# Reordering one DMA-issuing queue in a fused linear-attention and Mish-MLP kernel

## The chip, the cores and the metric

The kernel runs on one core of a Trainium2 chip. A core has a matrix engine (PE, TensorE), a vector engine (DVE, VectorE), an activation engine (ACT, ScalarE), a general engine (POOL, GpSimd) and an engine that here only issues transfers (SP, SyncE). Each engine works through its own queue of instructions in order; an instruction that needs a result of another engine or of a transfer (a DMA) waits at the head of its queue, and everything behind it on that engine waits as well. SP, ACT and POOL issue DMAs. The metric is the device time of one execution in microseconds.

## The reference

Attention with a per-head decay `lam`, computed block by block with a running state, and then a two-layer network. There are 4 batches, 8 heads, 768 positions and a head size of 64.

```python
for b in range(nb):
    sl = slice(b * block, (b + 1) * block)
    qb, kb, vb = (q[:, :, sl].copy(), k[:, :, sl].copy(), v[:, :, sl].copy())
    intra = np.einsum('bhic,bhjc->bhij', qb, kb) * Dmask[None]
    intra = np.einsum('bhij,bhjd->bhid', intra, vb)
    inter = np.einsum('bhid,bhde->bhie', qb * lam_pow[None], kv_state)
    out[:, :, sl] = intra + inter
    rev_pow = lam[:, None, None] ** (block - 1 - pos[None, :, None])
    kb_dec = kb * rev_pow[None]
    kv_state = lam_block[None, :, None, None] * kv_state + np.einsum('bhsd,bhse->bhde', kb_dec, vb)
...
h = x @ w_in
sp = np.where(h > 20.0, h, np.log1p(np.exp(np.minimum(h, 20.0))))
g = h * np.tanh(sp)
return (g @ w_out).astype(np.float32)
```

`x` holds the attention's output as 3072 tokens by 512 features; `w_in` is 512 x 2048 and `w_out` 2048 x 512. `g` is the Mish function of `h`.

## The kernel before, in words

**Stages.** The 768 positions are cut into NG = 6 groups of C = 128. Group n has B = 4 chunks, one for each batch, numbered i = 4n + b. Stage n of the main loop (line 800) does the two matrix layers for the 512 tokens of group n and, in between, the attention of group n + 1, in pairs of chunks: pair `s` (batches 0 and 1) and pair `t` (batches 2 and 3). Group 0 and the attention of group 1 are done ahead of that loop.

**Units.** A stage is a list of units of PE work written out by hand. For n > 1 there are 27: units 0 to 12 are the first layer (products `ph`, and for the last 1024 hidden features a scheme with seven half-size products, whose tiles appear as `sx`, `sz`, `sw`, `sy`), and units 13 to 26 are the second layer, in seven steps of two units each: P1 (13, 14), P5 (15, 16), P6 (17, 18), P2 (19, 20), P7 (21, 22), P3 (23, 24) and P4 (25, 26), with the tiles `x`, `w`, `z`, `x`, `z`, `y`, `z`. Stage 1 has 16 units of the first layer, so that its P1 is 16 and 17 and its P4 28 and 29. After each unit's PE work the loop body places other engines' work, in program order; this order is the order of each engine's queue.

**The path of one chunk.** `load_k`, `load_q` and `load_v` are DMAs issued by POOL (lines 66 to 78), one in each unit of `slots`, each behind a tiny copy (`pace`, line 408) that waits for the newest activation output. `scale_k` (line 262) multiplies a chunk of k by its decay on DVE and gives `ktil`. `turn` (line 269) calls `scale_k` and then issues two DMA transposes on SP: `qraw` from `qn` and `kraw` from `ktil`. `pair_s` (line 338) makes the scores of two chunks on PE (`pS`) and masks them on DVE (`sb`, line 365). `pair_o` (line 368) makes the outputs on PE and scales them into `xtok`: for pair `t` at once on DVE (line 385), for pair `s` later on ACT (line 389), from the list `scales`, whose four entries are taken in units 15, 16, 17 and 19. After the second half of each chunk's `xtok` SP issues the DMA transpose into `xt` (line 392), the input of the first layer in the next stage. `pair_a` (line 320) updates the running state (`raw`, line 288, and `state`, line 293).

**The readers of `xt`.** In stage n the units 0 to 3 use only the half of `xt[n]` that pair `s` gave. The half of pair `t` is first read by `x_sum(n, 0)` on DVE (line 519), placed in unit 3 ahead of `pair_s` on `s`, and by PE from unit 4 on.

**The stores.** P2 and P4 store through ACT's queue. P7 and P3 end in `plus` (line 651): DVE adds two halves into `osum` (line 654), and SP issues the store at once. The `osum` tiles rotate through 4 buffers (tag `osb`).

**Buffers that bear on the order.** `kn` has 6 buffers, `qn` 5, `ktil` 6, `qraw` and `kraw` 4 each.

**SP's queue in a stage with n = 2 or 3**, in program order: turns of chunks 4(n+1)+2 and 4(n+1)+3 (units 1 and 2); transposes into `xt` of pair `s` (units 16 and 19); turn of chunk 4(n+2) (unit 20); store of P7 (22); turn of chunk 4(n+2)+1 (23); store of P3 (24); transposes into `xt` of pair `t` (25). In stage 4 the turns of units 20 and 23 are absent, since there is no further group.

Of the kernel before, what the change touches and what calls it, by code (L numbers as in the profile page):

```python
# [13 lines left out]
def bc(ap, axis, n):  # L14
    shape = list(ap.shape)
    shape.insert(axis, n)
    return ap.unsqueeze(axis).broadcast_to(shape)
# [3 lines left out]
def kernel(  # L21
# [10 lines left out]
    nc = tc.nc  # L32
    B, H, S, D = q.shape
    C = 128
    NG = S // C
# [41 lines left out]
    def load_v(i):  # L77
        nc.gpsimd.dma_start(out=vz[i % NVB][:, :, 0:D], in_=chunk_rows(v, i))  # L78
# [119 lines left out]
    ktil = {}  # L198
# [27 lines left out]
    def look_s(i):  # L226

        kT, qT = kq[i]
        pS = [ps.tile([128, JP, C], F32, name="pS", tag=g, bufs=m)
              for g, m in (("pS", 1), ("po", 2) if i < B else ("pk", 1))]  # L230
        for j in range(JP):
            for t in range(2):
                rs = slice(64 * t, 64 * t + 64)
                nc.tensor.matmul(pS[t][:, j, :], kT[rs, j, :], qT[rs, j, :],
                                 start=(j == 0), stop=(j == JP - 1), skip_group_check=True)
        sbs[i] = [None, None]
        for t in (0, 1) if i < B else (1, 0):
            sbs[i][t] = work.tile([128, JP, C], F16, name="sb", tag="sb", bufs=4)
            nc.vector.tensor_tensor(out=sbs[i][t], in0=pS[t],
                                    in1=dm[:, t] if i < B else bc(maskT, 1, JP), op=ALU.mult)  # L240
# [21 lines left out]
    def scale_k(i):  # L262

        t = work.tile([128, H, D], F16, name="ktil", tag="ktil", bufs=6)
        (nc.gpsimd if B + 1 < i < 2 * B else nc.vector).tensor_tensor(  # L265
            out=t, in0=kn[i], in1=bc(lk, 2, D), op=ALU.mult)
        ktil[i] = t

    def turn(i):

        scale_k(i)
        for src, name, to in ((qn, "qraw", qraw), (ktil, "kraw", kraw)):
            to[i] = work.tile([128, JP, C], F16, name=name, tag=name, bufs=4)
            nc.sync.dma_start_transpose(out=to[i], in_=src[i].rearrange("p h c -> p (h c)"))
# [16 lines left out]
    def next_state(n, p):  # L291

        nc.vector.tensor_tensor(
            out=state[p][(n + 1) % 2], in0=raws[n, p],
            in1=lbc.unsqueeze(1).unsqueeze(3).broadcast_to([128, 2, JP, D]), op=ALU.mult)
# [112 lines left out]
    def pace():  # L408
        nc.gpsimd.tensor_copy(paced, mark[-1])  # L409
# [188 lines left out]
    def token_sum(n, i, part):  # L598

        if (n, i) not in gsum:  # L600
            gsum[n, i] = work.tile([128, HK, 2 * C], F16, name=f"gsum{i}", tag=f"gsum{i}", bufs=1)
        w = HK // 2
        ks = slice(part * w, part * w + w)
        kh = slice(HK + part * w, HK + part * w + w)
        h = hsg[n]
        lo, hi = slice(0, 2 * C), slice(2 * C, 4 * C)
        a, b, op = (
            lambda: (h[:, ks, hi], h[:, kh, hi], ALU.add),
            lambda: (gsum[n, 0][:, ks, :], h[:, ks, lo], ALU.subtract),
            lambda: (h[:, ks, lo], h[:, ks, hi], ALU.subtract),  # L610
            lambda: (h[:, kh, lo], gsum[n, 1][:, ks, :], ALU.subtract),
        )[i]()
        nc.vector.tensor_tensor(out=gsum[n, i][:, ks, :], in0=a, in1=b, op=op)  # L613
# [31 lines left out]
    def store(n, r, c, t, queue, blk=None, lo=0, hi=None):  # L645
        hi = HN if hi is None else hi
        b0, b1 = (2 * r, 2 * r + 2) if blk is None else (2 * r + blk, 2 * r + blk + 1)
        dst = out_v[n * C : (n + 1) * C, b0:b1, c * HN + lo : c * HN + hi]
        queue.dma_start(out=dst, in_=t)

    def plus(n, r, c, key):

        o = work.tile([128, 2, HN], F32, name="osum", tag="osb", bufs=4)
        nc.vector.tensor_tensor(out=o, in0=bank[n, key], in1=p5[n], op=ALU.add)  # L654
        store(n, r, c, o, nc.sync)

    p5 = {}
    u3 = []

# [140 lines left out]
    for n in range(1, NG):  # L800
        r, s, t = Pair(), Pair(), Pair()
        r.n, r.bs, s.n, s.bs, t.n, t.bs = n, (2, 3), n + 1, (0, 1), n + 1, (2, 3)
        def duo(g, half):
            return mm1_duo, (n, g, half * (GT // 2), (half + 1) * (GT // 2))

        def part(g, *steps):
            return [(set_unit, (n, g, step)) for step in steps]

        later = []
        if 1 < n < NG - 1:  # L810
            later += [lambda i=(n + 1) * B + b: load_v(i) for b in range(B)]
        if n < NG - 2:
            later += [lambda f=f, i=(n + 2) * B + b: f(i) for b in range(B) for f in (load_k, load_q)]
        if n == 1:
            units = [[duo(g, half)] for half in range(2) for g in range(NKI // 2)]
            visit = {11: (pair_s, s), 16: (pair_o, s), 21: (pair_a, s), 26: (pair_s, t), 29: (pair_o, t)}
            turns = {1: 9, 4: 10, 7: 11, 23: 12, 25: 13}
            slots = range(8, 16)
            sums = {9: ((2, 0),), 11: ((2, 1),), 13: ((0, 0), (1, 0)), 15: ((0, 1), (1, 1)), 20: ((3, 0),), 21: ((3, 1),)}
        else:  # L820
            units = [part(0, "P1") + part(1, "P1") + [duo(0, 0)], part(0, "P2") + part(1, "P2") + [duo(1, 0)],
                     [duo(2, 0)], [duo(3, 0)],
                     [duo(0, 1)], part(0, "open") + [duo(1, 1)], part(1, "open") + [(mm1_duo, (n, 2, GT // 2, GT, True))],
                     part(0, "P5") + [(duo_mish, (n, 2, 1))] + part(1, "P5"), part(0, "P6", "mid") + part(1, "P6"), [duo(3, 1)] + part(1, "mid"),
                     part(0, "P7") + part(1, "P7"), part(0, "P3") + part(1, "P3"),
                     part(0, "P4") + part(1, "P4") + part(0, "late") + part(1, "late")]
            if n == NG - 1:
                units[0] += units[1].pop(),
            visit = {}
            if n < NG - 1:  # L830
                visit = {0: (pair_a, r), 3: (pair_s, s), 13: (pair_o, s), 22: (pair_s, t), 25: (pair_o, t)}
            if n < NG - 2:
                visit[17] = pair_a, s
            turns = {1: (n + 1) * B + 2, 2: (n + 1) * B + 3, 20: (n + 2) * B, 23: (n + 2) * B + 1}
            slots = range(4, 16)
            sums = {9: ((2, 0),), 12: ((0, 0), (0, 1), (1, 0), (1, 1)), 14: ((2, 1),), 18: ((3, 0),), 19: ((3, 1),)}
        steps = ("P1", "P5", "P6", "P2", "P7", "P3", "P4")
        units += [[(fast_unit, (n, step, blk))] for step in steps for blk in range(2)]
        scales = []
        for u, calls in enumerate(units):  # L840
            for fn, args in calls:
                fn(*args)
            if n == 1 and u == 0:
                turn(8)
                look_s(7)
            if n == 1 and u == 2:
                f = look_kv(7)
                look_o(7)
                f()
                next_state(1, 1)  # L850
            for _ in range({0: 1, 1: 1, 2: 2, 3: 1, 4: 1}.get(u, 0) if n == 1 else 0):
                pace()
                ahead.pop(0)()
            if later and u in slots:
                pace()
                later.pop(0)()
            for i, part in sums.get(u, ()):
                token_sum(n, i, part)
            if turns.get(u, NG * B) < NG * B:
                turn(turns[u])  # L860
            if n > 1 and u == 3:
                x_sum(n, 0)
            if u in visit:
                f, s_ = visit[u]
                s_.spare = ("po", "po") if u < 13 else ("pS", "pk") if f is pair_a else ("ph", "po")
                if f is pair_o and s_ is s and n > 1:
                    f(s_, scales)
                else:
                    f(s_)
            if n > 1 and scales and u in (15, 16, 17, 19):  # L870
                scales.pop(0)()
            if n > 1 and u == 4:
                for i in range(1, 4):
                    x_sum(n, i)
# [30 lines left out]
```

## Time and profile before

| What | Value |
|---|---|
| Timed runs | 199.07, 199.34, 200.79 us (median 199.34) |
| The profiled execution's own time | 198.38 us |
| Its span in the profile | 196.6 us |
| PE idle, recorded waits from 57 to 196.6 us | one, 0.3 us |
| SP, waits of stores for `osum` | 69.5 us in 6, the longest 41.9 |
| DVE, waits of `xsum` for the DMA into `xt` | 4.3 us in 2, the longest 3.6 |

The span is what the profile covers, from the first instruction to the last; the execution's own time has 1.78 us around it. SP's waits are the waits of an issuing queue, which are free unless something behind the waiting transfer is needed. How to read the rows of the profile: a timeline row has the start and the duration in us, the engine (SPq is SP's queue, with issue time as its duration), the line of the kernel, the operation, the output tile and its inputs, the shapes, how many instructions the row merges, and in brackets the idle time ahead of it and what ended that. A row on landing gives the smallest, middle and largest time from a DMA's issue until its data is there.

### The profile page before, as it was taken

What the parts mean: (1) busy time and instruction counts of PE and PEld (TensorE: products, weight loads), DVE (VectorE), ACT (ScalarE), POOL (GpSimd) and SP (SyncE); (2) the same over time, 40 slices, a digit from 0 to 9 for tenths busy, and PEclk for the clock granted to TensorE, in tenths of its full rate; (3) what the DMA queues carried; (4) which work ended last, traced back from release to release, by engine and by line L of the source; (5) the groups of instructions that cost most, each with busy time, mean ns of one, the idle gap of its engine ahead of it and who ended that gap; (6) DMA issues with size and microseconds to landing.
All of it is one profiled execution on the core that took longest, in us unless ns stands there. A gap on an engine that the chain in (4) does not pass through costs nothing.

```text
span 196.6 us, 5100 instructions
## 1 busy us (share of the span) xinstructions
PE 189.4 (96%) x2049; PEld 157.8 (80%) x2049; DVE 145.2 (74%) x279; ACT 110.7 (56%) x230; POOL 78.7 (40%) x129
## 2 busy tenths in 40 slices
PE   7978999999999999999999999999999999999993
PEld 3654447978888998988998988998987988888882
DVE  8789689899944978898769798769788728227813
ACT  5695674333665521567880657980647880787520
POOL 7996333679487800008970008960007000000000
PEclk9999999999999999999999999999999999999999
DMA  8999999999999997759999959999969914600014
GB/s 127 141 144 200 207 205 207 155 174 212 198 128 161 179 137 170 182 89 94 129 120 196 216 107 111 121 122 159 218 136 103 62 27 137 160 3 2 0 57 160
DMA packets 112458, 26.82 MB, mean 136 GB/s; under 512 B 101554, under 2 KB 112434, under 8 KB 112434
## 3 DMA queue, kind: packets, MB, share of 16 engines
q0 software_dynamic: 77552, 13.37, 93.2%
q1 hardware_dynamic: 30848, 9.97, 28.8%
q10 hardware_dynamic: 4034, 3.15, 5.7%
q8 instruction: 16, 0.26, 0.6%
q14 instruction: 8, 0.07, 0.1%
HBM read 27.26 MB, written 6.29 MB: 171 GB/s over the span
## 4 chain that ended last, share of the span: by engine, by line
PE 74%; DMA 11%; POOL 8%; DVE 4%; issue 1%; ACT 1%; POOLq 0%; DVEq 0%; ACTq 0%
PE ph L453 19%; PE z L627 14%; DMA wout<-in_moe_w_out_dram 10%; PE x L627 9%; PE y L627 6%; PE sz L579 5%; PE w L627 4%; PE sx L579 3%; PE pS L349 2%; PE pO L376 2%; POOL win L93 2%; POOL vz L78 2%; PE sy L579 2%; PE sw L579 2%; POOL kn L67 1%; POOL qn L75 1%
## 5 line engine op out<-in xcount | busy, mean ns | idle before, releaser
L453 PE MATMUL ph<-xt,win 128*128 128x256 f16 x384 | 45.0, 273 | 0.0
L453 PEld LDWEIGHTS <-win 128*128 128x128 f16 x384 | 37.1, 98 | 5.0 <-issue 0.2
L627 PEld LDWEIGHTS <-gsum 128*128 128x128 f16 x384 | 36.9, 98 | 4.5
L465 ACT ACTIVATE hsg<-ph 128x512 f16<-128x512 f32 x48 | 28.6, 596 | 14.8 <-PE ph L453 14.6
L409 POOL COPY paced<-hsg 1x1 f16<-1x1 f16 x42 | 9.8, 234 | 55.3 <-ACT hsg L465 55.3
L627 PEld LDWEIGHTS <-hsg 128*128 128x128 f16 x272 | 26.0, 98 | 3.2
L627 PE MATMUL x<-wout,hsg 128*128 128x256 f16 x192 | 23.7, 273 | 0.0
L627 PE MATMUL z<-tsum,gsum 128*128 128x256 f16 x192 | 23.6, 273 | 0.0
L613 DVE TENSOR_TENSOR gsum<-hsg 128x1024 f16<-128x1024 f16 x24 | 16.1, 686 | 9.6 <-ACT hsg L540 4.7
L78 POOL DMA_DIRECT2D vz<-in_v_dram x24 | 21.1, 881 | 4.9 <-DMA wout<-in_moe_w_out_dram 1.7
L67 POOL DMA_DIRECT2D kn<-in_k_dram x23 | 20.5, 892 | 6.1 <-DMA win<-in_moe_w_in_dram 2.2
L75 POOL DMA_DIRECT2D qn<-in_q_dram x23 | 20.4, 885 | 6.0 <-DMA wout<-in_moe_w_out_dram 3.6
L365 DVE TENSOR_TENSOR sb<-pS,maskT 128x512 f16<-128x512 f32 x32 | 19.8, 682 | 0.5 <-PE pS L349 0.3
L684 ACT ACTIVATE osum<-z 128x512 f32<-128x512 f32 x5 | 3.0, 597 | 25.1 <-PE z L627 25.1
L265 DVE TENSOR_TENSOR ktil<-kn,lk 128x512 f16<-128x512 f16 (+1 forms) x22 | 14.6, 683 | 2.2 <-DMA kn<-in_k_dram 2.2
L288 DVE TENSOR_TENSOR raw<-pv,state 64x256 f32<-64x256 f32 x24 | 10.1, 422 | 7.8 <-PE pv L328 7.4
L418 PE MATMUL ph<-xt,win 128*128 128x512 f16 x64 | 14.5, 379 | 0.3 <-ACT xt L257 0.3
L579 PEld LDWEIGHTS <-isum 128*128 128x128 f16 x128 | 12.5, 98 | 2.0 <-issue 0.5
L430 ACT ACTIVATE hsg<-ph 128x512 f16<-128x512 f32 x16 | 9.6, 597 | 5.8 <-PE ph L418 5.8
L418 PEld LDWEIGHTS <-win 128*128 128x128 f16 x64 | 6.1, 98 | 7.3 <-DMA win<-in_moe_w_in_dram 0.5
L654 DVE TENSOR_TENSOR osum<-z,p 128x512 f32<-128x512 f32 x6 | 4.1, 690 | 10.6 <-issue 5.9
L627 PE MATMUL y<-wout,gsum 128*128 128x256 f16 x96 | 11.8, 273 | 0.0
(113 smaller groups left out, 314.6 us busy)
## 6 DMA issues: line engine op xcount, KB each, us to landing
vz<-in_v_dram POOLq DMA_DIRECT2D x24, 128.0 KB, 4.6
out_dram<-osum SPq DMA_DIRECT2D x12, 256.0 KB, 3.3
kn<-in_k_dram POOLq DMA_DIRECT2D x23, 128.0 KB, 5.3
qn<-in_q_dram POOLq DMA_DIRECT2D x23, 128.0 KB, 5.9
out_dram<-osum ACTq DMA_DIRECT2D x11, 256.0 KB, 3.1
wout<-in_moe_w_out_dram POOLq DMA_DIRECT2D x4, 512.0 KB, 16.4
win<-in_moe_w_in_dram POOLq DMA_DIRECT2D x3, 512.0 KB, 10.1
win<-in_moe_w_in_dram POOLq DMA_DIRECT2D x2, 256.0 KB, 6.2
```

What stands on the lines that cost most here:

```text
L67: nc.gpsimd.dma_start(out=kn[i], in_=chunk_rows(k, i))
L75: nc.gpsimd.dma_start(out=qn[i], in_=chunk_rows(q, i))
L78: nc.gpsimd.dma_start(out=vz[i % NVB][:, :, 0:D], in_=chunk_rows(v, i))
L265: (nc.gpsimd if B + 1 < i < 2 * B else nc.vector).tensor_tensor(out=t, in0=kn[i], in1=bc(lk, 2, D), op=ALU.mult)
L288: nc.vector.tensor_tensor(out=raw[rs, b % 2, j0 : j0 + nj, :], in0=pv[rs, :, rs], in1=olds(rs), op=ALU.add)
L365: nc.vector.tensor_tensor(out=s.sb[m][t], in0=sc[m][t], in1=bc(maskT, 1, JP), op=ALU.mult)
L418: nc.tensor.matmul(ph_t[ni][:, lo:hi], w_in(ni, kc), xt[n][:, kc, lo:hi], start=(kc == 0), stop=(kc == NKC - 1),)
L453: nc.tensor.matmul(t[:, m, lo - half * h : hi - half * h], w_in(ni, kc), xt[n][:, kc, lo:hi], start=(m == 0 and kc == 0), stop=(kc == NKC ...
L465: nc.scalar.activation(dst, duo_t[n, g, half], AF.Mish)
L579: nc.tensor.matmul(t[:, m, :], lhs(kk, m), rhs(kk), start=(step in ("P1", "P5") and m == 0 and kk == 0), stop=(kk == KH - 1), skip_group_c ...
L613: nc.vector.tensor_tensor(out=gsum[n, i][:, ks, :], in0=a, in1=b, op=op)
L627: nc.tensor.matmul(places(n, key)[:, blk, lo:hi], lhs(kk, blk), rhs(kk, lo, hi), start=(fresh and kk == 0 and blk == 0), stop=(kk == HK - ...
```

## The change

- `turn` no longer scales k if the chunk was scaled already.
- In stages 1 to 4 the stores of P7 and P3 are put on a list, `owed`, and issued at the end of the body of unit 25 (unit 29 in stage 1), behind `pair_o` of pair `t` and so behind its two transposes into `xt`. Stages 0 and 5 keep the old order.
- The loads of group n + 2 come in the order k, k, q, q for batches 0 and 1 and then for 2 and 3, instead of k, q, k, q.
- The turns of the next group's first pair move from units 23 and 25 to 20 and 22 in stage 1, and from 20 and 23 to 19 and 20 in stages 2 and 3.
- In stages 2 and 3 `scale_k` of that pair is placed in unit 15, both chunks together.
- The entries of `scales` are taken ahead of the turn and the visit of their unit instead of behind them, so that in unit 19 the last transpose into `xt` of pair `s` still comes ahead of the turn.

```diff
     def turn(i):
-        scale_k(i)
+        if i not in ktil:
+            scale_k(i)
...
         nc.vector.tensor_tensor(out=o, in0=bank[n, key], in1=p5[n], op=ALU.add)
-        store(n, r, c, o, nc.sync)
-
+        if 0 < n < NG - 1:
+            owed.append(lambda: store(n, r, c, o, nc.sync))
+        else:
+            store(n, r, c, o, nc.sync)
+
+    owed = []
...
         if n < NG - 2:
-            later += [lambda f=f, i=(n + 2) * B + b: f(i) for b in range(B) for f in (load_k, load_q)]
+            later += [lambda f=f, i=(n + 2) * B + b + c: f(i)
+                      for b in (0, 2) for f in (load_k, load_q) for c in range(2)]
...
-            turns = {1: 9, 4: 10, 7: 11, 23: 12, 25: 13}
+            turns = {1: 9, 4: 10, 7: 11, 20: 12, 22: 13}
...
-            turns = {1: (n + 1) * B + 2, 2: (n + 1) * B + 3, 20: (n + 2) * B, 23: (n + 2) * B + 1}
+            turns = {1: (n + 1) * B + 2, 2: (n + 1) * B + 3, 19: (n + 2) * B, 20: (n + 2) * B + 1}
...
                 token_sum(n, i, part)
+            if n > 1 and scales and u in (15, 16, 17, 19):
+                scales.pop(0)()
+            if n > 1 and u == 15 and n < NG - 2:
+                scale_k((n + 2) * B)
+                scale_k((n + 2) * B + 1)
             if turns.get(u, NG * B) < NG * B:
                 turn(turns[u])
...
-            if n > 1 and scales and u in (15, 16, 17, 19):
-                scales.pop(0)()
+            if u == (29 if n == 1 else 25):
+                while owed:
+                    owed.pop(0)()
```

## The prediction, made before the change was run

> **What bounds the kernel now.** I read the page's busy times and slices first, to learn which engine is full, then busy time by stage, then the chain of waits around the one stage that differs from its neighbours, and last the queues of SP, DVE and POOL there.
>
> ```profile
> span 196.6 us, 5100 instructions
> PE 189.4 (96%) x2049; PEld 157.8 (80%) x2049; DVE 145.2 (74%) x279; ACT 110.7 (56%) x230; POOL 78.7 (40%) x129
> PE   7978999999999999999999999999999999999993
> ...
> 80.50:109.60 29.10, 29.10 (x347) 25.86 (x345) 23.89 (x46) 17.88 (x43) 12.50 (x24) 1.00 1.34 143
> 109.60:138.65 29.05, 29.05 (x346) 25.82 (x345) 23.55 (x45) 18.19 (x43) 12.39 (x24) 1.00 1.52 141
> 138.65:167.90 29.25, 28.87 (x339) 25.38 (x337) 20.58 (x40) 17.98 (x43) 4.57 (x8) 1.00 0.71 105
> ```
>
> TensorE (PE) is busy in every slice from the fourth to the last but one, and the granted clock is 1.00 in the stretches. The three stretches are the stages n = 2, 3 and 4; columns are length, then busy time of PE, weight load, DVE, ACT, POOL, then the granted clock. Stages 2 and 3 have no PE idle time at all. Nothing that SP, DVE or POOL does can make a stage shorter than PE's own work, and the change takes no PE instruction away. So the whole possible gain is the PE time lost in stages 1 to 4. Stage 4 has 0.38 us of it (29.25 - 28.87), although it has less to do: it has no state update for the next pair (`pair_a` on `s` stands only where n < 4). To size the loss I compare like with like, from each stage's first matmul (`sx`) to the first product of the second half (`x`), which hold the same units in stages 3 and 4. The columns of the chain of waits are start, duration, what:
>
> ```profile
> 109.59 0.87 PE sx L579 x8
> ...
> 124.15 0.87 PE x L627 x8
> ...
> 138.65 0.87 PE sx L579 x8
> ...
> 142.55 2.45 DMA xt<-xtok
> ...
> 147.53 0.60 ACT sz L559
> 148.13 0.52 ACT hsg L465
> 148.70 0.60 PE sw L579 x4
> ...
> 153.84 0.87 PE x L627 x8
> ```
>
> Stage 3 takes 124.15 - 109.59 = 14.56 us, stage 4 takes 153.84 - 138.65 = 15.19: **0.63 us lost**. The chain names the path: the second half of `xt` is transposed by a DMA that lands at 145.00 (142.55 + 2.45), `x_sum` on DVE waits for it, the four masked scores `sb` are queued behind `x_sum`, ACT's copy `sz` waits for the bank that `sb` reads, the Mish `hsg` is queued behind that copy, and PE's `sw` waits for the bank that this Mish empties.
>
> **The change part by part.** *Stores behind the outputs' transposes, and the next pair's transposes in one piece (turns at units 19 and 20).* SP's queue at the end of stage 3, and the DVE work that feeds it:
>
> ```profile
> 133.54 1.20 SPq L274 DMA_TRANSPOSE qraw<-qn  x1
> ...
> 136.15 0.54 SPq L649 DMA_DIRECT2D out_dram<-osum  x1
> 136.79 1.22 SPq L274 DMA_TRANSPOSE qraw<-qn  x1
> 138.10 1.21 SPq L274 DMA_TRANSPOSE kraw<-ktil  x1
> 139.40 1.75 SPq L649 DMA_DIRECT2D out_dram<-osum  x1
> 141.25 2.52 SPq L392 DMA_TRANSPOSE xt<-xtok  x2
> ...
> 138.09 1.40 DVE L385 TENSOR_TENSOR xtok<-pO,lqt 128x256 f16<-128x256 f32 x4
> ...
> 143.05 1.28 DVE L265 TENSOR_TENSOR ktil<-kn,lk 128x512 f16<-128x512 f16 x2
> 145.09 0.42 DVE L519 TENSOR_TENSOR xsum<-xt 128x512 f16<-128x512 f16 x1 [0.76 <-DMA xt<-xtok]
> 145.55 2.48 DVE L365 TENSOR_TENSOR sb<-pS,maskT 128x512 f16<-128x512 f32 x4
> ```
>
> The first `xtok` is ready after two of DVE's four, at about 138.09 + 0.70 = 138.79, but SP issues its transpose at 141.25: it stands behind a transpose that ends at 139.31 and a store that takes 1.75. After the change SP runs four transposes in a row from 133.54, each about 1.3 from start to start (136.79 to 138.10), so the fourth ends at about 133.54 + 3 x 1.3 + 1.21 = 138.65. The outputs' transposes then start at 138.8 and 140.1 instead of 141.25 and 142.55, that is 2.45 us sooner. With the landing of 2.45 from the chain, `xt` is there at about 142.55. DVE gets to `x_sum` when `ktil` ends, 143.05 + 1.28 = 144.33, so the wait is gone with 1.8 us to spare.
>
> What is late next is `sb`. In stage 3, where `x_sum` waits for nothing, it starts as soon as PE has written the scores:
>
> ```profile
> 115.20 0.62 PE L349 MATMUL pS<-qraw,kraw 64*128 64x128 f16 x16
> 144.27 0.62 PE L349 MATMUL pS<-qraw,kraw 64*128 64x128 f16 x16
> ...
> 115.86 2.48 DVE L365 TENSOR_TENSOR sb<-pS,maskT 128x512 f16<-128x512 f32 x4
> ```
>
> There `sb` starts 0.66 after the first score matmul; in stage 4 that would be 144.93 instead of 145.55, 0.62 sooner. That is the 0.63 by another road, and beyond it PE sets the start. So this term is **-0.63 us**, in stage 4 alone: in stages 2 and 3 PE loses nothing now. The two stores cost SP the same issue time later, behind the outputs' transposes; queued behind them are only the transposes for units 1 and 2 of the next stage, whose scores PE reads at unit 22. In stage 4 that is well after the `x` of unit 13 at 153.84, while SP is done with `xt` at 143.77 (141.25 + 2.52) even now: over 10 us of cover for a delay of 1 or 2. Each stage takes four `osum` buffers and there are four, so a store held back to unit 25 is waited for by the same step one stage on. Cost 0.
>
> *k decays moved, k ahead of q.* In stages 2 and 3 the two `scale_k` go from units 20 and 23 to unit 15 on DVE. No instruction is added. The stage 2 rows:
>
> ```profile
> 97.98 0.68 DVE L613 TENSOR_TENSOR gsum<-hsg 128x1024 f16<-128x1024 f16 x1
> 100.18 1.75 DVE L288 TENSOR_TENSOR raw<-pv,state 64x256 f32<-64x256 f32 x4 [1.51 <-PE pv L328]
> ...
> 102.57 1.29 DVE L613 TENSOR_TENSOR gsum<-hsg,gsum 128x1024 f16<-128x1024 f16 x2
> 103.78 0.68 DVE L265 TENSOR_TENSOR ktil<-kn,lk 128x512 f16<-128x512 f16 x1
> ...
> 93.44 0.87 POOL L67 DMA_DIRECT2D kn<-in_k_dram  x1
> 94.42 0.87 POOL L75 DMA_DIRECT2D qn<-in_q_dram  x1
> 95.69 0.88 POOL L67 DMA_DIRECT2D kn<-in_k_dram  x1 [0.23 <-issue]
> ...
> DMA to landing us min/median/max: 4.1/4.3/4.9
> ```
>
> DVE is idle for 1.51 us before `raw`, and the two decays (1.28 for a pair, by the `ktil` row above) fit into it: 98.6 to 99.9, ahead of 100.18. The new wait is for the loads. The first k is issued at 93.44 as before; the second takes q's slot at 94.42 instead of 95.69. The last row above is the k loads' time to landing in stage 2 (4.1 to 4.9), so they are there by 98.3 and 99.3, when DVE comes for them or before. With the old order the second would land at up to 100.6 and hold `raw`. Queued behind the wait on DVE are `raw`, the state and `gsum`, and PE needs that `gsum` for step P3. Cost 0, bounded above in the second rival; below, two instructions leave a stretch of DVE that is full (103.78 on), which saves nothing on PE's path. At n = 1 the turns only come sooner (units 20 and 22) and their decays fall into DVE's idle time ahead of `raw` and `osum` of that stage: 0. ACT's scaled outputs keep their order on ACT and on SP (they are popped ahead of the turn of unit 19 instead of ahead of that of unit 20): 0.
>
> **The sum.** -0.63 + 0 + 0 = -0.63. The profiled execution took 198.38 us (span 196.6 and 1.78 around it) and becomes 197.75. The three timed runs have their median at 199.34, 0.96 above the profiled one, with the same program, so I take the same difference off it: **198.7**.
>
> **Rivals.** *First: the transposes land no sooner.* Landing, not issue, may be the limit, since six transposes now follow each other with an ACT store beside them. The rows for the outputs' transposes (from 80 to 170 us) and for the q transposes issued at 133.54 and 136.79:
>
> ```profile
> DMA to landing us min/median/max: 2.4/2.5/3.4
> ...
> DMA to landing us min/median/max: 4.9/4.9/4.9
> ```
>
> At 4.9 the second output transpose, issued at 140.1, lands at 145.0, exactly as now, and the gain is 0: 199.3. From 4.2 down (144.3) the gain is whole. All the output transposes so far landed within 3.4, those right behind a store among them, which speaks for the gain; that q's took twice as long while the DMA engines were loaded speaks for the rival. The Trainium skill has a rule on this side (DMA: Bandwidth & Descriptors, "Issuing engines are not separate DMA queues"): DMAs from all queues run on the same 16 engines and interleave, and starting them from several queues saves only issue time. Taken strictly, with the engines full, a sooner issue lands no sooner and the sum is 0; the landings of 2.4 to 3.4 behind a store lean against that reading here. Chance 0.25.
>
> *Second: DVE stands at the early decays (slower).* If the second k lands late, DVE holds everything behind it. After the landing come the decay (0.60, half of a pair less its overlap), `raw` and the state (102.57 - 100.18 = 2.39) and two `gsum` (1.29), 4.3 us together, and PE wants the last of it in the first P3 product, which runs from 105.52:
>
> ```profile
> 105.52 1.85 PE y L627 x16
> ```
>
> Half of that product's 0.9 needs only the first `gsum`, so the deadline is about 105.9 and the k must be there by 101.6, 7.2 us after its issue at 94.42. The latest k in stage 3 took 6.6:
>
> ```profile
> DMA to landing us min/median/max: 4.0/4.3/6.6
> ```
>
> so no k load of these stages would have reached that point; each us beyond it costs PE one, in stage 2 and again in stage 3. The weights' loads early in the run took longer:
>
> ```profile
> win<-in_moe_w_in_dram POOLq DMA_DIRECT2D x3, 512.0 KB, 10.1
> ```
>
> At the 10.1 of that row the loss would be 2 x 2.9 = 5.8 and the time 199.34 - 0.63 + 5.8 = 204.5; at 8.7 it would be 3.0, or 201.7. No weights are loaded in these stages, so chance 0.07.
>
> *Third: timed runs lose more than the profiled one.* They lie between 199.07 and 200.79; if the excess is the same wait for `xt` recurring in other stages, the change takes off up to the 199.34 - 198.38 = 0.96 as well, 0.63 + 0.96 = 1.6 in all: 197.8. Nothing in the profile shows such waits (stages 2 and 3 are full). Chance 0.08, with 0.03 of it for more than that, as only the slowest timed run lies far enough above the profiled one (2.41) to hold it.
>
> **How the numbers follow.** The forecast, 198.7, has 0.60; no gain, 199.3, 0.25; slower by DVE's wait 0.07; the larger gain 0.08. The range runs from the larger gain, 197.8, to 200.3, which is no gain plus two thirds of what the slowest timed run lies above the median (1.45), as medians of few runs move. That leaves out the slow rival and the far end of the larger gain, about 1 in 10, and some of the runs' own spread. About 1% (2 us) is what a measurement of this kernel can tell from no change. Faster by over 1% needs under 197.35, a gain of 2.0 where the profile has 0.63 to give: 0.03. Slower by over 1% is the second rival, 0.07. Within 1%: 0.90.
>
> **What would show it.** Right: on SP four transposes in a row from about 133.5, `xt` issued near 138.8, both stores behind; no DVE wait of `xsum` for `xt` in stage 4, no PE wait of `sw` there, and sx to x in 14.56. For the k decays: two `ktil` ahead of `raw` in stages 2 and 3, with at most tenths of idle time for the loads. Wrong: `xt` landing 4 us or more after its issue, DVE idle on `kn` for over 2 us, or a PE wait in a stage that has none now.

## The result, and the profile after

| | Median | Runs | Range |
|---|---|---|---|
| Kernel before | 199.17 us | 19 | 198.14 to 201.58 |
| Changed kernel | 198.46 us | 19 | 197.63 to 199.40 |

The ratio is 0.9956, with a 95% interval of 0.9936 to 0.9977: the change takes off 0.9 us, with 0.5 to 1.3 us inside the interval. The ratio leaves out the run of 201.58 us, which counts as a slow one; the medians differ by 0.71 us. The forecast was 198.7 us, a gain of 0.63; the measured median lies 0.24 us below it.

The profiled execution of the changed kernel took 198.19 us (span 196.4). Its page says the same of PE as before, one percentage point fuller:

```profile
span 196.4 us, 5097 instructions
PE 189.9 (97%) x2049; PEld 158.3 (81%) x2049; DVE 144.8 (74%) x279; ACT 110.8 (56%) x230; POOL 79.0 (40%) x129
```

By this page the span fell by only 0.2 us. The stages tell where the rest is. The view of busy time by stretches, cut at each stage's first `sx`, has length, then busy time of PE, weight load, DVE, ACT and POOL, then the granted clock:

```profile
80.99:110.06 29.07, 29.07 (x347) 25.84 (x345) 24.46 (x48) 17.85 (x43) 12.71 (x24) 1.00 1.35 143
110.06:139.12 29.06, 29.06 (x346) 25.80 (x345) 23.58 (x46) 18.17 (x43) 12.60 (x24) 1.00 1.48 143
139.12:167.75 28.63, 28.63 (x339) 25.41 (x337) 20.03 (x39) 18.02 (x43) 4.46 (x8) 1.00 0.68 101
```

Stages 2 and 3 are as long as before. Stage 4 took 29.25 us (138.65 to 167.90) and now takes 28.63, with no idle time of PE left in it: 0.62 us gained (29.25 - 28.63). Against that, this execution reached stage 2 at 80.99 us, where the profile of before had 80.52: 0.47 us lost in the part before it. The tail of stage 5 gives 0.05, and -0.62 + 0.47 - 0.05 is the -0.20 of the span. The part ahead of stage 2 varies by itself: two profiles of the kernel before reached stage 2's first `sx` at 80.52 and 81.41, two of the changed kernel at 80.99 and 80.55. So one pair of spans says little here, and the stages' own lengths say much.

In the chain of waits (start, duration, what) the half of stage 4 from `sx` to `x` is now as long as that of stage 3, 14.57 us each, and no DMA, DVE or ACT step stands between the two in stage 4:

```profile
110.06 0.87 PE sx L580 x8
...
124.63 0.87 PE x L628 x8
...
139.12 0.87 PE sx L580 x8
...
153.69 0.87 PE x L628 x8
```

The timelines of SP's queue and of DVE at the same place (line numbers of the changed kernel are one higher around here):

```profile
134.60 1.20 SPq L275 DMA_TRANSPOSE qraw<-qn  x1
136.30 1.20 SPq L275 DMA_TRANSPOSE kraw<-ktil  x1
137.61 1.19 SPq L275 DMA_TRANSPOSE qraw<-qn  x1
138.90 1.22 SPq L275 DMA_TRANSPOSE kraw<-ktil  x1
140.21 3.19 SPq L393 DMA_TRANSPOSE xt<-xtok  x2
143.45 1.09 SPq L650 DMA_DIRECT2D out_dram<-osum  x2
...
143.52 1.29 DVE L265 TENSOR_TENSOR ktil<-kn,lk 128x512 f16<-128x512 f16 x2
144.74 0.43 DVE L520 TENSOR_TENSOR xsum<-xt 128x512 f16<-128x512 f16 x1
145.40 2.48 DVE L366 TENSOR_TENSOR sb<-pS,maskT 128x512 f16<-128x512 f32 x4 [0.23 <-PE pS L350]
```

Four transposes run in a row (with 0.50 us between the first two), both stores stand behind the outputs' transposes, `xsum` follows `ktil` with no wait for a DMA, and `sb` waits for PE's scores and for nothing else. But the two output transposes take 3.19 us of SP where they took 2.52. The first alone holds SP for 1.88, and the second starts at 142.18:

```profile
140.21 1.88 SPq L393 DMA_TRANSPOSE xt<-xtok  x1
...
142.18 1.22 SPq L393 DMA_TRANSPOSE xt<-xtok  x1
```

The early decays stand where they were meant to, in the idle time ahead of `raw`, with no wait for a load (DVE in stage 2):

```profile
99.06 1.29 DVE L265 TENSOR_TENSOR ktil<-kn,lk 128x512 f16<-128x512 f16 x2
100.65 0.42 DVE L289 TENSOR_TENSOR raw<-pv,state 64x256 f32<-64x256 f32 x1 [0.30 <-PE pv L329]
```

### The profile page after: what moved, and what is told of

The parts are those of the page before. It is cut to its first block, busy times and chain, and to the rows that moved or that the text cites. A ratio compares the mean times of both kernels' runs of the same rounds, so it can differ in the third digit from the quotient of the medians.

```text
span 196.4 us, 5097 instructions
## 1 busy us (share of the span) xinstructions
PE 189.9 (97%) x2049; PEld 158.3 (81%) x2049; DVE 144.8 (74%) x279; ACT 110.8 (56%) x230; POOL 79.0 (40%) x129
## 4 chain that ended last, share of the span: by engine, by line
PE 93%; ACT 2%; DVE 2%; issue 1%; ACTq 0%
PE ph L454 22%; PE z L628 15%; PE x L628 11%; PE ph L419 7%; PE y L628 6%; PE sz L580 5%; PE w L628 5%; PE sx L580 4%; PE pS L350 2%; PE pO L377 2%; PE pO L255 2%; PE sy L580 2%; PE sw L580 2%; PE pS L234 1%; PE pv L329 1%; PE busy L157 1%
```

## The experiments

Theory A is the prediction's: SP's issue of two stores ahead of the outputs' transposes holds `xt`, which reaches PE through DVE's queue in stage 4, and nothing else in the change matters. Theory B gives the gain to the earlier turns and decays. Theory C says that timed runs lose more than the profile shows. Ratios are to the kernel before, run on the same chip between the others.

### One part alone: the stores held back

```diff
-        store(n, r, c, o, nc.sync)
+        if 0 < n < NG - 1:
+            owed.append(lambda: store(n, r, c, o, nc.sync))
+        else:
+            store(n, r, c, o, nc.sync)
...
+            if u == (29 if n == 1 else 25):
+                while owed:
+                    owed.pop(0)()
```

> The kernel before with one part of the change alone: the stores of P7 and P3 are held back behind the outputs' transposes in stages 1 to 4. Theory A (SP's issue of the two stores ahead of the outputs' transposes is the whole cost): without them the transposes into xt go out 1.5 to 2.5 us sooner, stage 4 from its first sx to its first x takes 14.6 instead of 15.19 us, PE has no wait in stage 4, and the ratio to the kernel before is about 0.997 (-0.6 us). Theory B (the earlier turns and decays make the gain): stage 4 keeps its 15.2 and the ratio is 1.000.

Measured: ratio 0.9985 (0.9964 to 1.0006), median 198.53 against 198.93. In its chain of waits stage 4 runs from 139.37 to 153.94:

```profile
139.37 0.87 PE sx L579 x8
...
153.94 0.87 PE x L627 x8
```

That is 14.57 us, and PE has no wait in stage 4: this part alone brings stage 4 to the length that the whole change gives it. The outputs' transposes start 0.33 us after the stage's `sx`, where they started 2.60 after it before (141.25 - 138.65) and 1.09 after it in the changed kernel (140.21 - 139.12):

```profile
139.70 3.45 SPq L392 DMA_TRANSPOSE xt<-xtok  x2
```

The timed ratio allows for no gain as well as for 0.63 us (0.997); the stage decides it.

### All parts but that one

```diff
-        if 0 < n < NG - 1:
-            owed.append(lambda: store(n, r, c, o, nc.sync))
-        else:
-            store(n, r, c, o, nc.sync)
+        store(n, r, c, o, nc.sync)
```

> The changed kernel with the stores of P7 and P3 issued at once, as before: turns, decays and order of loads stay changed. Theory A: SP gets through its four transposes sooner but still issues two stores ahead of the transposes into xt, the second with about 1.75 us; stage 4 from sx to x takes 15.0 to 15.2 us and the ratio to the kernel before is 0.999 to 1.000. Theory B: 14.6 us and 0.997.

Measured: ratio 1.0014 (0.9991 to 1.0038). Stage 4 takes 154.42 - 138.94 = 15.48 us, and stage 3, which lost nothing before, takes 124.43 - 109.69 = 14.74:

```profile
109.69 0.87 PE sx L580 x8
...
124.43 0.87 PE x L628 x8
...
138.94 0.87 PE sx L580 x8
...
154.42 0.87 PE x L628 x8
```

Theory B falls: without the stores held back, stage 4 keeps its loss. In this one profile the other parts even lose more than the kernel before did, 0.29 us in stage 4 and 0.17 in stage 3, which the timed ratio can't tell from no change. With both transposed chunks issued early, the two stores come together, right ahead of the outputs' transposes, and the first of those goes out 2.87 us after `sx`, later than before:

```profile
138.10 1.23 SPq L275 DMA_TRANSPOSE kraw<-ktil  x1
139.41 2.30 SPq L650 DMA_DIRECT2D out_dram<-osum  x2
141.81 2.54 SPq L393 DMA_TRANSPOSE xt<-xtok  x2
```

### The path through DVE's queue

```diff
-            if n > 1 and u == 3:
-                x_sum(n, 0)
             if u in visit:
...
                 else:
                     f(s_)
+            if n > 1 and u == 3:
+                x_sum(n, 0)
```

> The kernel before with one line moved: x_sum(n, 0) stands behind the masked scores of pair s in unit 3 instead of ahead of them. SP's queue is untouched, so xt lands as late as before (145.0 in the profile of before). Theory A says that the loss reaches PE only by way of DVE's queue (x_sum holds the masked scores): then stage 4 takes 14.6 to 14.7 us and the ratio is about 0.997. If late outputs reach PE in another way (through unit 4, which reads them, or through SP), stage 4 keeps about 15.2 us and the ratio is 1.000.

Measured: ratio 0.9987 (0.9964 to 1.0009). SP's queue is as before (both stores ahead, the outputs' transposes from 141.85), yet stage 4 takes 153.78 - 139.14 = 14.64 us:

```profile
141.85 2.53 SPq L392 DMA_TRANSPOSE xt<-xtok  x2
...
145.42 2.49 DVE L365 TENSOR_TENSOR sb<-pS,maskT 128x512 f16<-128x512 f32 x4 [0.59 <-PE pS L349]
147.82 0.41 DVE L519 TENSOR_TENSOR xsum<-xt 128x512 f16<-128x512 f16 x1
...
139.14 0.87 PE sx L579 x8
...
153.78 0.87 PE x L627 x8
```

The late `xt` costs next to nothing once the scores no longer stand behind `xsum`: in the profile 0.55 (15.19 - 14.64) of the 0.62 us come back without a change to SP. So the loss went by way of DVE's queue, as the chain of waits had it.

### A third store ahead

```diff
-            store(n, 0, 0, o, nc.scalar)
+            store(n, 0, 0, o, nc.sync if 0 < n < NG - 1 else nc.scalar)
```

> The kernel before with the suspected cost raised by half: in stages 1 to 4 P2's store is issued by SP instead of ACT, so that a third store stands ahead of the transposes into xt. Theory A: each store costs SP 0.54 to 1.75 us, xt comes that much later, stage 4 takes 15.7 to 16.9 us, and stage 3, whose x_sum had no slack, loses 0.5 us or more too: ratio 1.005 to 1.012. If landing and not issue decides, nothing moves: 1.000.

Measured: ratio 1.0041 (1.0020 to 1.0063), so +0.8 us, somewhat under what was expected. Most of its loss isn't where it was expected: stage 2 takes 96.04 - 81.29 = 14.75 us, stage 3 125.51 - 110.54 = 14.97 and stage 4 155.22 - 140.01 = 15.21. Stages 2 and 3 lose 0.18 and 0.40 us that they did not lose before; stage 4 loses what it lost before. SP's rows ahead of stage 4 show why it loses no more:

```profile
135.25 0.53 SPq L649 DMA_DIRECT2D out_dram<-osum  x1
...
141.76 0.78 SPq L649 DMA_DIRECT2D out_dram<-osum  x1
142.63 2.52 SPq L392 DMA_TRANSPOSE xt<-xtok  x2
```

A store more takes 0.53, but the last one now takes 0.78 instead of 1.75, and `xt` goes out 2.62 us after `sx`, where it was 2.60. The 1.75 is not the price of a store. In stages 2 and 3 `x_sum` now waits for `xt`, where the profile of before records no wait, so the loss there comes the same way:

```profile
87.30 0.43 DVE L519 TENSOR_TENSOR xsum<-xt 128x512 f16<-128x512 f16 x1 [0.33 <-DMA xt<-xtok]
...
116.77 0.42 DVE L519 TENSOR_TENSOR xsum<-xt 128x512 f16<-128x512 f16 x1 [0.54 <-DMA xt<-xtok]
```

### Both kernels again

These two are the changed kernel and the kernel before, without an edit.

> The changed kernel once more, to see how far its gain repeats and whether it goes beyond holding the stores back. Theory A (the stores are all of it): the ratio is that of the stores alone, about 0.997 to 0.9985. Theory C (the other parts add 0.3 us or more in timed runs, which the first profile doesn't show): 0.9956 again, or lower. The profile has stages 2, 3 and 4 at 14.56 to 14.6 us from sx to x under both.

> The kernel before against itself: what a ratio of no change looks like, and a second profile of it. Both theories: 0.999 to 1.001. Theory A: stages 2 and 3 at 14.56 to 14.6 us from sx to x, stage 4 at 14.9 to 15.5. Theory C': in some executions stage 3 loses 0.2 us or more too, which would make the mean loss larger than the 0.63 of the first profile.

Measured: the changed kernel 0.9982 (0.9954 to 1.0011), the kernel before against itself 1.0012 (0.9986 to 1.0039). The first repeats the gain only as a tendency, and the second shows that a ratio of these runs moves by 0.001 with no change of the kernel. The stages are clearer: the changed kernel has 14.56 to 14.57 us in stages 2, 3 and 4 once more, and the kernel before has 14.56 and 14.57 in stages 2 and 3 and 154.54 - 139.54 = 15.00 in stage 4, a loss of 0.43 where the first profile had 0.62. Neither theory C nor C' shows in a profile: neither profiled execution of the kernel before lost time in stage 3. That doesn't refute theory C, which is about timed runs: the interval of the repeat still holds 0.9956.

The second profile of the kernel before, with the others, allows one more comparison. Wherever `x_sum` stands ahead of the scores and waits for `xt`, the chain of waits has the landing of `xt` (start plus duration). These are the rows of the kernel before run again in stage 4, of the kernel without the stores held back in stage 4, and of the third store in stages 3 and 4:

```profile
143.25 2.46 DMA xt<-xtok
...
143.12 2.46 DMA xt<-xtok
...
114.18 2.49 DMA xt<-xtok
...
143.93 2.45 DMA xt<-xtok
```

From the landing to the stage's `x` it is 154.54 - 145.71 = 8.83 us, 154.42 - 145.58 = 8.84, 125.51 - 116.67 = 8.84 and 155.22 - 146.38 = 8.84, and in the first profile of the kernel before 153.84 - 145.00 = 8.84. A stage without loss takes 14.57 us, so `xt` may land up to 14.57 - 8.84 = 5.73 us after `sx` at no cost; in these five stages each us beyond that cost one. In the first profile of the kernel before it landed 145.00 - 138.65 = 6.35 us after `sx`, which is the whole loss of 0.62.

### The loads in the old order

```diff
-            later += [lambda f=f, i=(n + 2) * B + b + c: f(i)
-                      for b in (0, 2) for f in (load_k, load_q) for c in range(2)]
+            later += [lambda f=f, i=(n + 2) * B + b: f(i) for b in range(B) for f in (load_k, load_q)]
```

> The changed kernel with the loads in the old order k, q, k, q and the early decays kept. The second k is then issued about 1.3 us later and lands at about 100.0 to 100.6 on the first profile's clock, after DVE comes for it at 99.2. By the prediction's count DVE stands 0.5 to 1.5 us in stages 2 and 3, raw starts up to 0.9 us later, and PE loses nothing, because the k may be as late as 101.6: stages 2 and 3 keep 14.5 us from x to the next sx and the ratio is that of the changed kernel. If DVE had no such slack, each stage would lose 0.5 to 0.9 us: 1.001 to 1.005.

Measured: ratio 0.9965 (0.9936 to 0.9993). DVE stands 0.46 us for the second k in stage 2 (0.56 in stage 3) and starts `raw` right after it:

```profile
100.10 0.69 DVE L265 TENSOR_TENSOR ktil<-kn,lk 128x512 f16<-128x512 f16 x1 [0.46 <-DMA kn<-in_k_dram]
100.71 1.74 DVE L289 TENSOR_TENSOR raw<-pv,state 64x256 f32<-64x256 f32 x4
```

Stages 2, 3 and 4 keep 14.57 us, and stages 2 and 3 in full keep 29.06 and 29.07: the wait costs nothing. Loading k ahead of q takes away a wait that costs nothing here.

### The loads so late that they must cost

```diff
-            later += [lambda f=f, i=(n + 2) * B + b + c: f(i)
-                      for b in (0, 2) for f in (load_k, load_q) for c in range(2)]
+            later += [lambda f=f, i=(n + 2) * B + b: f(i) for f in (load_q, load_k) for b in range(B)]
```

> The changed kernel with all four q of the next group loaded ahead of the four k. The second k then takes the sixth slot (99.0 on the first profile's clock) and with 4.0 to 5.0 us to landing is there at 103.0 to 104.0, 1.4 to 2.4 us past the point, 101.6, from which the second rival's loss should begin. By that count stages 2 and 3 lose 1.4 to 2.4 us each between x and the next sx and the time grows by 2.8 to 4.8 us over the changed kernel, to about 201.3 to 203.3. If the deadline was drawn too early, the loss is under 1 us.

Measured: median 204.29 us, ratio 1.0266 (1.0226 to 1.0306), or 5.8 us over the changed kernel's 198.46; more than expected. From the first `x` to the next stage's `sx`, 14.50 us before (109.59 - 95.09), stage 2 takes 16.93 and stage 3 18.57:

```profile
96.47 0.87 PE x L628 x8
...
113.40 0.87 PE sx L580 x8
...
127.96 0.87 PE x L628 x8
...
146.53 0.87 PE sx L580 x8
```

DVE's rows for stage 2, and the second decay of stage 3:

```profile
104.67 0.69 DVE L265 TENSOR_TENSOR ktil<-kn,lk 128x512 f16<-128x512 f16 x1 [0.43 <-DMA kn<-in_k_dram]
...
109.59 2.47 DVE L366 TENSOR_TENSOR sb<-pS,maskT 128x512 f16<-128x512 f32 x4
...
137.80 0.69 DVE L265 TENSOR_TENSOR ktil<-kn,lk 128x512 f16<-128x512 f16 x1 [2.37 <-DMA kn<-in_k_dram]
```

The second decay starts 104.67 - 96.47 = 8.20 us after `x` in stage 2 and costs 16.93 - 14.50 = 2.43; it starts 137.80 - 127.96 = 9.84 after it in stage 3 and costs 4.07. Both give the same point from which time is lost: 8.20 - 2.43 = 5.77 and 9.84 - 4.07 = 5.77 us after `x`. Beyond it each us costs one, as the second rival had it. On the clock of the profile of before the point is 95.09 + 5.77 = 100.86, where the prediction had 101.6. PE's rows show what the prediction left out:

```profile
111.52 0.41 PE L377 MATMUL pO<-vz,sb 128*128 128x64 f16 x8 [0.16 <-DVE sb L366]
```

Behind `gsum`, DVE still has to do an `osum` and the four masked scores of pair `t`, and PE's outputs wait for these last. In both stages DVE's rows follow each other from the second decay to these scores with gaps of at most 0.1 us. (The chain of waits of stage 3 names the landing of a q transpose at 142.73 ahead of the scores. The scores of pair `t` don't read it, and they follow `osum` by 0.61 us in both stages, so it held nothing.) The size was missed by that, and by the loads themselves, of which the second k of stage 3 took 5.8 us, not 4 to 5.

### What is left

```diff
-                     part(0, "P5") + [(duo_mish, (n, 2, 1))] + part(1, "P5"), part(0, "P6", "mid") + part(1, "P6"), [duo(3, 1)] + part(1, "mid"),
+                     [(duo_mish, (n, 2, 1))] + part(0, "P5") + part(1, "P5"), part(0, "P6", "mid") + part(1, "P6"), [duo(3, 1)] + part(1, "mid"),
```

> The changed kernel with one more line moved, to test what is left of PE's waits in stages 2 to 4: in unit 7 the Mish that empties the bank of unit 9's product stands ahead of the first P5 instead of between the two. In the changed kernel that product takes 1.00 us where an undisturbed one takes 0.87, since ACT copies P5's p first. If this copy is the cause, stages 2, 3 and 4 take 14.44 us from sx to x instead of 14.57, about 0.4 us in all, and the ratio to the kernel before is some 0.002 below that of the changed kernel (0.994 to 0.997). If DVE's wait for p then comes late, sx to x stays at 14.57 or grows.

Measured: ratio 0.9955 (0.9931 to 0.9979), no different from the changed kernel's, and 14.62 to 14.63 us in stages 2, 3 and 4 instead of 14.57. Unit 9's product takes 0.88 from start to start (121.27 - 120.39) and the one behind it 1.02 (122.29 - 121.27):

```profile
120.39 1.04 PE L454 MATMUL ph<-xt,win 128*128 128x256 f16 x8
121.27 1.18 PE L580 MATMUL sz<-xsum,isum 128*128 128x256 f16 x8
122.29 1.04 PE L580 MATMUL sy<-xsum,win 128*128 128x256 f16 x8
```

The wait only moved to the next product, and it grew. No kernel tried here is faster than the changed one by more than the noise.

## Why the prediction was right

- **What bounds the kernel.** That PE's own lost time is all there is to gain held: with stage 4's loss gone, its stretch is full, and no experiment brought a stage below the 14.56 us that stage 3 had before.
- **The term of -0.63.** The profile has -0.62 in stage 4. In time, the first comparison gives -0.9 (-0.5 to -1.3) and the repeat -0.4 (-0.9 to +0.2); 0.63 lies in both. That holding the stores back carries it is shown by the two complementary experiments, and that it goes through DVE's queue by moving `x_sum`. The fixed 8.84 us from the landing to `x` in five stages that lost time shows it too.
- **How much sooner `xt` goes out.** This number inside the term was too large. The prediction had the outputs' second transpose 2.45 us sooner, 1.45 us after the stage's `sx` (140.1 - 138.65), and 1.8 us to spare for `x_sum`. It went out 142.55 - 138.65 = 3.90 us after `sx` before and 142.18 - 139.12 = 3.06 in the changed kernel: 0.84 us sooner. Of the 1.61 us missing, 0.94 is that the first output transpose started late, 1.09 after `sx` instead of 0.15: the four transposes ahead of it began 0.59 us later against `sx` than before (134.60 - 139.12 against 133.54 - 138.65), behind pair `s`'s transposes, and had a gap of 0.50 between the first two. The other 0.67 is that the first output transpose held SP. The prediction took the 1.75 us of the second store for that store's own price; 1.21 of it (1.75 - 0.54) was a hold that, 0.66 long, fell on this transpose instead (1.88 - 1.22). In the changed kernel run again the first output transpose started 0.16 after `sx`, as predicted, and was held for 2.23 us, so that the second went out 2.49 after `sx`. So the hold recurs, and the late start does not.
- **Why 0.63 held all the same.** PE can get back no more than it lost, and for that `xt` had to land 6.35 - 5.73 = 0.62 us sooner. With the 2.5 us that the second transpose takes to land, it was there about 5.5 us after `sx`, some 0.2 to spare, and about 5.0 in the run again. The cap was worked out; that 0.84 was enough was in part luck.
- **The stores' cover, and the turns in one piece.** The later stores cost nothing, as said. The earlier turns were costed at nothing too. Without the stores held back they lost 0.29 and 0.17 us in the one profile taken, with the second output transpose 0.28 us later in stage 4 than before (143.12 - 138.94 against 3.90); in the changed kernel they cost nothing.
- **The decays and the loads.** Zero was right, and the old order of loads would have been free as well, with 0.46 us of DVE's wait. The second rival is a real mechanism with the price of one for one, but its point lay 0.7 us sooner than counted, because `osum` and the masked scores were left out of the chain behind the load. In the changed kernel the second decay starts at about 99.06 + 0.61 = 99.67, 4.1 us after `x` (95.56), against 5.77.
- **The first rival** (landing decides, no gain) did not come true, yet the margin was thin, through SP's hold and the late start and not through the landing: the second output transpose landed 2.5 us after its issue, as before. The prediction's sign against itself, a landing 4 us or more after the issue, did show for the first output transpose in the run again (4.6 us, with 2.23 of issue), at no cost, as it was there 4.8 us after `sx`. **The third** is neither shown nor excluded: the first interval allows for more than 0.63 us, and no profile shows where more would come from. The two near copies of the changed kernel, with the old loads and with the Mish first, gave 0.9965 and 0.9955.

## What to carry to other kernels

Before pricing a transfer in an issuing queue, look at where its issue time is longer than that of its like: that excess may belong to the place in the queue and pass to whoever takes it, so moving the long one away may not free its whole length. Follow a late transfer to the engine that pays: here it was a vector instruction standing ahead of scores it had nothing to do with, and in the profile moving that one line in DVE's queue did nearly as much as reordering SP's. Where a landing is suspected, subtract it from the end of the stage in several runs: a constant difference shows the path and how late is too late. For a gain under 1%, compare stage lengths between fixed instructions of the bound engine; the spans carry the spread of the other stages.

## What the runs showed of the hardware that was not expected

SP's issue of one DMA in a series is sometimes held far beyond its usual time, at roughly the same point and not for a given instruction. At the end of stage 3 the hold is on the second store before (1.75 us where the first took 0.54), on the first output transpose after the change (1.88 where the one ahead of it took 1.22), and nearly gone when a third store stands in the queue (0.78 for the last). In all eleven profiles the issue that SP is at 2.0 us after stage 4's `sx` is longer than its like and ends between 2.3 and 3.0 us after `sx`, whatever it is and wherever it started. What it waits for, the trace doesn't name. In each of these profiles ACT issues P4's store 0.66 to 0.67 us after the same `sx`; that store, and the DMAs already in flight, are guesses that no run here tested.
